# A planned attention and mixture kernel: the order of issue read from a table, and other engines for the last evictions

## The chip, the cores and the metric

The kernel runs on one core of a Trainium2 chip. The metric is the device time of one execution in microseconds (us), taken as the median of several runs; lower is better.

## The reference

Two parts follow each other. The first is attention over B = 8 batches, 8 heads, 576 positions and 64 elements a head. It is the sum of a full attention over queries, keys and values averaged over groups of four positions (144 of them, each result repeated four times), and a banded attention in which a position sees only those less than four away:

```
out_d    = softmax(scale * q_d @ k_d^T) @ v_d        # q_d, k_d, v_d: means over 4 positions
out_up   = repeat(out_d, 4)
scores   = where(|i - j| < 4, scale * q @ k^T, -1e9)
x        = (out_up + softmax(scores) @ v)  as (4608, 512)
```

The second part takes x (4608 tokens of 512) through four matrices:

```
out = ((x @ w1) * (x @ w2)) @ w3 @ w_out     # w1, w2: 512x1024, w3: 1024x1024, w_out: 1024x512
```

The four weight matrices arrive as 64-bit floating-point words.

## The kernel before

**The weights.** A weight block is loaded as raw 64-bit words (`raw`, 512 KB a load) and turned into 32-bit numbers on chip: ScalarE writes the high part (L355) and mostly also prepares the low one (L363; in a part of the blocks VectorE does it, L367), VectorE joins them (L370). w3 and w_out are multiplied once at the start: `product(m, j)` (into `accw`, L408) builds the folded matrix `wphl`, kept as a high and a low part (L429, L430). In the listings, `wo` is w_out, and `w_163`, `w_174`, `w_229` and so on are blocks of w3. `gate_block` converts w1 and w2 in the same way and splits them (L466, L468).

**The matmuls of the second part.** A product of numbers split in high and low is made with three matmuls (`three`, L323 to L325). `moe(c)` handles a chunk of 384 tokens, twelve chunks in all. For each of eight f blocks, four tasks of six matmuls give the two gates in `pab`; ScalarE copies the first (`a`, L1010), VectorE multiplies it with the second (L1012), ScalarE and VectorE split the result (`gh` L1017, `gl` L1019), and three tasks of three matmuls (`down`) add it to three accumulators `acc`. At the chunk's end ScalarE evicts the accumulators into `o_sb` (L1029), and SyncE's queue stores them (L1044 or L1046). In the last chunk ScalarE evicts the first half of each accumulator's columns, VectorE the second half (L1031), and the middle store is issued from ScalarE's queue.

**The attention.** The tokens come in 24 units of 192. For batches 0 and 1 (`group_unit`, `group_scores`, `group_values`) TensorE computes the banded scores. For the others `unit(n)` works on VectorE and ScalarE: loads of q, k and v (`q_t`, `kv`), seven shifted products (`pr`, L863) and their sums (`s_t`, L876 on VectorE, L873 on ScalarE), a softmax, seven weighted values (`pv`), added up in `xl` by VectorE (L940) or by an accumulating DMA from GpSimd's queue (L938). The pooled attention is `pooled_sums` or `pooled` (which loads averages with further accumulating DMAs from GpSimd, L505), then `quad`: scores on TensorE (`s_ps`, L566), softmax (`pexp`, L581 to L600), a turn on TensorE (`t_ps`, `pt`, L609 to L618) and the values (`o_ps`, L527). The unit's result is split into `xh` and `xl` for the gates.

**What sets the order.** Every step is recorded as a task by `Plan.add`, with its engine, an assumed cost, its dependencies and the buffers (rings) that it takes and uses. `Plan.order` then simulates the engines with these costs, forwards and backwards, many times, keeps the best sequence, shifts the priorities of some groups by a list of numbers (`SHIFTS`), and returns one global order. The program is emitted in it, and each engine executes its own tasks strictly in that order. The three DMA queues used are those of SyncE, GpSimd and, once at the end, ScalarE. A load on SyncE's queue waits, by the semaphores it is given in turn, for the one issued eight loads before it. The first four weight loads are put ahead of all other loads by `AHEAD`.

Of the kernel before, what the change touches and what calls it, by code (L numbers as in the profile page):

```python
# [20 lines left out]
DM, DF = 512, 1024  # L21
# [21 lines left out]
NC = NU // 2  # L43
# [16 lines left out]
DEPTH = dict(PE=0.0)  # L60
SLACKS = (0.0, 0.1, 0.3, 0.6)
SLOW = [(slow, spare) for spare in (0.22, 0.5) for slow in (1.0, 1.1, 1.2)]
VARY = 0.03
RARE = 0.003
SEEDS = 4
ROUNDS = 8
AHEAD = 4

SHIFTS = [
    "gates.8.2:2 gates.9.5:-15.5",  # L70
    "down.0.1:-10 down.0.4:21.5 down.0.5:47.5 down.0.7:-65 down.1.1:-12 down.1.5:2 down.11.2:-4.5 down.2.0:-1"
    " down.2.2:-2 down.2.3:-11.5 down.2.4:-7.5 down.2.5:-46.5 down.3.2:-14.5 down.3.3:8.5 down.3.6:-11"
    " down.3.7:-29.5 down.4.4:-7 down.4.6:-10 down.5.4:14 down.6.4:-36 down.6.5:5 down.6.6:2.5 down.6.7:-52"
    " down.7.4:-19 down.7.7:1.5 down.8.4:3.5 down.8.5:74 down.9.2:3 down.9.3:-24 gate_block.0.0.0:-5.5"
    " gate_block.0.1.0:-21 gate_block.0.1.1:-15.5 gate_block.1.0.2:-20.5 gate_block.1.1.0:-26.5"
    " gate_block.1.1.2:-6.5 gates.0.0:-14 gates.0.1:-4 gates.0.2:-3.5 gates.0.5:-6 gates.1.1:1 gates.1.3:2"
    " gates.1.6:-2.5 gates.2.0:4.5 gates.2.1:-11.5 gates.2.2:2.5 gates.2.3:-3 gates.2.4:-3 gates.2.5:0.5"
    " gates.3.1:-7 gates.3.2:-30 gates.3.5:-31 gates.3.7:-16.5 gates.4.0:-20.5 gates.4.1:-29 gates.4.2:-14"
    " gates.4.4:1.5 gates.5.2:3.5 gates.5.3:0.5 gates.5.6:-3 gates.5.7:-1.5 gates.6.0:2 gates.6.2:-19.5 gates.6.3:-2"
    " gates.6.6:-1 gates.7.1:1.5 gates.7.6:-0.5 gates.8.3:2.5 gates.8.7:3 gates.9.6:-31.5 group_scores.0.2.0:4"  # L80
    " group_scores.0.2.1:3.5 group_scores.1.0.1:4.5 group_scores.1.1.0:-3 group_values.1:-14 group_values.2:3"
    " out_weight.3:-1 out_weight.4:3 out_weight.6:14 part.6.1:10.5 pooled.0:2.5 pooled.1:4.5 pooled.3:5.5"
    " pooled.4:3.5 pooled.6:11 pooled_sums.1:2.5 product.4.5:-6 product.7.0:7 product.7.1:4 quad.1.0:10.5"
    " quad.2.0:-6 quad.2.1:1 quad.3.0:-4.5 quad.3.1:-1 quad.4.0:1.5 quad.4.1:1 quad.6.0:0.5 quad.7.0:-7.5 rest.0:-1"
    " rest.1:-21.5 unit.11:-1 unit.13:1 unit.14:1 unit.16:1 unit.17:-4.5 unit.20:0.5 unit.21:2 unit.22:-0.5"
    " unit.23:7 unit.6:-1 unit.7:-0.5",
]
# [24 lines left out]
class Plan:  # L112
# [28 lines left out]
    def link(self):  # L141
        at = {t: i for i, t in enumerate(self.tasks)}
        self.pre, self.suc, self.then = [], [[] for _ in self.tasks], [[] for _ in self.tasks]
        for i, t in enumerate(self.tasks):
            l = sorted({at[d] for d in t.deps} | {at[d] for r in t.rings for d in r} - {i})
            self.pre.append(l)
            for d in l:
                self.suc[d].append(i)
            for d in t.after:
                self.then[at[d]].append(i)  # L150

    def run(self, prio, slack, back=False, slow=1.0, spare=0.22):


        tasks = self.tasks
        pre, suc = (self.suc, self.pre) if back else (self.pre, self.suc)
        n = len(tasks)
        left, can = [len(l) for l in pre], [0.0] * n
        if not back:
            left = [a + len(t.after) for a, t in zip(left, tasks)]  # L160
        start, end, order = [0.0] * n, [0.0] * n, []
# [1019 lines left out]
```

## Time and profile before

| | us |
|---|---|
| median of three runs | 768.3 |
| the runs | 767.92, 768.3, 769.8 |
| profiled execution, span | 769.4 |
| TensorE busy (PE) | 741.0 |
| VectorE busy (DVE) | 618.4 |
| ScalarE busy (ACT) | 524.4 |
| GpSimd busy (POOL) | 153.2 |

For the profiled execution the page gives its span alone, from the first to the last instruction; no other time of it is recorded. Busy times are sums over an engine's instructions; weight loads of TensorE (PEld) run beside its matmuls. Times in the rows of the profile are counted from the start of the span. In a row of instructions, the brackets at the end give the idle time of the engine in front of it, and what ended it. SPq, ACTq and POOLq are the DMA issues of SyncE, ScalarE and GpSimd. The profiled execution is 1.1 us longer than the median.

### The profile page before, as it was taken

To read this page: it belongs to the slowest core of one execution; us is meant where nothing else is said; L and a number is where in the kernel's file an instruction comes from. 1 tells how busy PE (TensorE), PEld (TensorE's weight loads), DVE (VectorE), ACT (ScalarE), POOL (GpSimd) and SP (SyncE) were. 2 spreads that over 40 slices of the span, in tenths; PEclk is the share of its full clock that TensorE was granted. 3 is DMA by queue.
4 is the path that set the end of the run, shared out by engine and by line. 5 is a ranking of instruction groups with operands and counts; after the bars stand their busy time and mean duration, and the time that the engine had idled before them with its cause. 6 is when DMAs were issued, how large, how long until landed. Compare 5 with 4: busy or idle time off the path is not lost.

```text
span 769.4 us, 14989 instructions
## 1 busy us (share of the span) xinstructions
PE 741.0 (96%) x5248; PEld 639.5 (83%) x5248; DVE 618.4 (80%) x1079; ACT 524.4 (68%) x2074; POOL 153.2 (20%) x187
## 2 busy tenths in 40 slices
PE   4989999999999999999999899999999999999996
PEld 1435578889988999899998798999997998999995
DVE  5567887658999999999996999999989999973111
ACT  4579689557877877877787687776786886842211
POOL 1120031301012412141030422420223320100000
PEclk9999999999999999999999999999999999999998
DMA  8896768515249757876469568764469544331101
GB/s 305 286 273 203 231 143 212 111 36 195 52 125 237 147 126 200 156 155 179 88 153 208 91 169 216 131 177 118 100 167 223 118 115 124 66 78 21 42 1 41
DMA packets 46051, 111.91 MB, mean 145 GB/s; under 512 B 6280, under 2 KB 12424, under 8 KB 45976
## 3 DMA queue, kind: packets, MB, share of 16 engines
q0 software_dynamic: 15360, 38.94, 29.6%
q1 hardware_dynamic: 30480, 71.75, 28.6%
q8 instruction: 41, 0.67, 0.4%
q14 instruction: 34, 0.28, 0.1%
q10 hardware_dynamic: 136, 0.26, 0.1%
HBM read 80.26 MB, written 9.44 MB: 117 GB/s over the span
## 4 chain that ended last, share of the span: by engine, by line
PE 79%; DMA 8%; DVE 6%; ACT 4%; issue 2%; POOL 0%; ACTq 0%; SPq 0%; DVEq 0%; POOLq 0%
PE pab L323 15%; PE pab L325 15%; PE pab L324 15%; PE acc L323 8%; PE acc L324 7%; PE acc L325 7%; DMA raw<-in_w_dram 4%; PE accw L408 4%; DMA kv<-in_kw_dram 2%; PE o_ps L527 1%; DVE pr L863 1%; PE s_ps L566 1%; PE t_ps L609 1%; ACT junk L873 1%; DMA xl<-pv 1%
## 5 line engine op out<-in xcount | busy, mean ns | idle before, releaser
L873 ACT ACTIVATE junk<-pr 128x64 f32<-128x64 f32 x432 | 111.1, 257 | 23.1 <-DVE pr L863 12.1
L863 DVE TENSOR_TENSOR pr<-q_t,kv 128x768 f32<-128x768 f32 x126 | 119.6, 967 | 4.1 <-DMA kv<-in_kw_dram 3.7
L922 ACT ACTIVATE pv<-kv,s_t 128x64 f32<-128x64 f32 x432 | 110.9, 338 | 11.5 <-DVE s_t L899 5.9
L323 PE MATMUL acc<-wphl,gh 128*128 128x512 f32 x288 | 114.4, 397 | 0.0
L325 PE MATMUL acc<-wphl,gl 128*128 128x512 f32 x288 | 113.2, 393 | 1.2 <-DVE gl L1019 1.2
L324 PE MATMUL acc<-wphl,gh 128*128 128x512 f32 x288 | 112.7, 391 | 0.0
L938 POOL DMA_DIRECT2D xl<-pv x54 | 48.3, 895 | 298.5 <-DVE xl L940 211.2
L1010 ACT COPY a<-pab 128x384 f32<-128x384 f32 x96 | 45.8, 477 | 71.6 <-PE pab L325 56.2
L1012 DVE TENSOR_TENSOR a<-pab,a 128x384 f32<-128x384 f32 x96 | 53.1, 553 | 48.2 <-PE pab L325 46.4
L876 DVE TENSOR_REDUCE s_t<-pr 128x12 f32<-128x768 f32 x90 | 84.1, 946 | 0.4
L1017 ACT CAST gh<-a 128x384 fp32r<-128x384 f32 x96 | 48.9, 510 | 47.3 <-PE acc L324 41.2
L873 ACT ACTIVATION_READ_ACCUMULATOR junk<-pr 128x1 f32 x432 | 81.1, 188 | 0.0
L408 PE MATMUL accw<-wo,w 128*128 128x512 f32 x128 | 64.5, 642 | 13.4 <-DVE w L370 12.8
L1019 DVE TENSOR_TENSOR gl<-a,gh 128x384 fp32r<-128x384 f32 x96 | 54.2, 566 | 27.6 <-ACT gh L1017 25.9
L930 DVE TENSOR_TENSOR pv<-kv,s_t 128x768 f32<-128x768 f32 x72 | 69.5, 969 | 0.1
L323 PE MATMUL pab<-xh,w1a 128*128 128x384 f32 x192 | 66.1, 344 | 2.2 <-ACT a L1010 1.9
L323 PE MATMUL pab<-xh,wb 128*128 128x384 f32 x192 | 65.4, 341 | 2.3 <-ACT a L1010 2.2
L323 PE MATMUL pab<-xh,wo 128*128 128x384 f32 x192 | 65.9, 343 | 0.0
L323 PE MATMUL pab<-xh,w2a 128*128 128x384 f32 x192 | 65.3, 340 | 0.3 <-DVE a L1012 0.3
L325 PEld LDWEIGHTS acc<-wphl,gl 128*128 128x128 f32 x288 | 54.0, 188 | 13.5 <-DVE gl L1019 1.6
L324 PE MATMUL pab<-xl,w1a 128*128 128x384 f32 x192 | 64.9, 338 | 0.2 <-DVE xl L810 0.2
L325 PE MATMUL pab<-xh,wo 128*128 128x384 f32 x192 | 64.8, 337 | 0.0
(118 smaller groups left out, 1726.8 us busy)
## 6 DMA issues: line engine op xcount, KB each, us to landing
xl<-pv POOLq DMA_DIRECT2D x54, 384.0 KB, 4.3
raw<-in_w_dram SPq DMA_DIRECT2D x32, 512.0 KB
qks<-in_qk_dram POOLq DMA_DIRECT2D x18, 576.0 KB, 7.6
kv<-in_kw_dram SPq DMA_DIRECT2D x18, 576.0 KB
kv<-in_vw_dram SPq DMA_DIRECT2D x18, 576.0 KB
out_dram<-o_sb SPq DMA_DIRECT2D x29, 256.0 KB
q_t<-in_q_dram SPq DMA_DIRECT2D x18, 384.0 KB
raw<-in_wout_dram SPq DMA_DIRECT2D x8, 512.0 KB
```

The costliest lines, as they stand in the source:

```text
L323: nc.tensor.matmul(out_ps, lhsT=lh, rhs=rh, start=first, stop=False)
L324: nc.tensor.matmul(out_ps, lhsT=lh, rhs=rl, start=False, stop=False)
L325: nc.tensor.matmul(out_ps, lhsT=ll, rhs=rh, start=False, stop=last)
L408: nc.tensor.matmul(accs[m], lhsT=T["x"][:, j % 4 * 128:j % 4 * 128 + 128], rhs=wo[0][:, j], start=j == 0, stop=j == NF - 1)
L863: (nc.gpsimd if o in share["qk_pool"] else nc.vector).tensor_tensor(out=T[o], in0=T["q"], in1=T["k"][:, o * D:o * D + nq].rearrange("p (t ...
L873: nc.scalar.activation(out=junk, in_=T[o][:, t], func=AF.Copy, accum_out=T["s"][:, t, o:o + 1])
L876: reds.append(add("DVE", dve_us(nq), lambda o=o: nc.vector.tensor_reduce(out=T["s"][:, :, o], in_=T[o], op=ALU.add, axis=AX.X), [tp], uses ...
L922: nc.scalar.mul(out=T["pv", o][:, tt], in_=T["v"][:, (tt + o) * D:(tt + o + 1) * D], mul=T["s"][:, tt, o:o + 1])
L930: nc.vector.tensor_tensor(out=T["pv", o], in0=T["v"][:, o * D:o * D + nq].rearrange("p (t d) -> p t d", d=D), in1=T["s"][:, :, o].unsqueez ...
L1012: tg = add("DVE", dve_us(CT), lambda f=f: nc.vector.tensor_tensor(out=T["a", f], in0=T["p", 1, f], in1=T["a", f], op=ALU.mult), [ta, ends[ ...
L1017: nc.scalar.copy(out=T["gh", f], in_=T["a", f])
L1019: tl = add("DVE", dve_us(CT), lambda f=f: nc.vector.tensor_tensor(out=T["gl", f], in0=T["a", f], in1=T["gh", f].bitcast(F32), op=ALU.subtr ...
```

## The change

The search is gone. A table, `ORDER`, holds for each engine the sequence in which it takes its tasks, as numbers into the list of tasks that the plan recorded for that engine; `order` merely merges the five sequences. `AHEAD` is gone too, but the table keeps the first four weight loads in front. In `moe`, the eviction of an accumulator depends on the last matmul into that accumulator (`ended[i]`), where it was the last into the third for all; the three evictions are recorded ahead of the three stores. In the last chunk the first and third accumulators are evicted whole by ScalarE, the second whole by VectorE, and the middle store, still on ScalarE's queue, also waits for the third eviction, and so is issued behind it.

```diff
-AHEAD = 4
-SHIFTS = [
-    "gates.8.2:2 gates.9.5:-15.5",
...
+ORDER = dict(
+    ACT=(
+        "76 75 78 77 79 81 80 82-83 0 2-3 84 1 86 6 85 5 87-88 7 4 8-9 89 91 90 93 92 10 13 12 14-15 11 94 18 16-17 21 20 19 96 95 97-98 "
...
     def order(self):
+
+        self.link()
+        mine, left, free, end, dma, order = {}, {}, {}, {}, 0.0, []
...
+        while any(left.values()):
+            can = []
+            for e in sorted(left):
+                if left[e] and all(j in end for j in self.pre[left[e][-1]] + self.begun[left[e][-1]]):
+                    can.append((max([free[e]] + [end[j] + (0.22 if self.tasks[j].eng == "PE" else LATENCY) for j in self.pre[left[e][-1]] if self.tasks[j].eng != e]), e))
+            s, e = min(can)
+            i = left[e].pop()
...
             if t.late:
+                dma = max(dma, free[e] + 1.3) + t.late
+                end[i] = dma + 0.8
+            order.append(t)
+        return order
...
+                ended[i] = lastd
...
+        last = c == NC - 1
+        kept = []
         for i in range(3):
-            def store_h(i=i):
+            def keep(i=i):
                 T["o", i] = pools["mp"].tile([128, DM], F32, name="o_sb", bufs=BUFS["o"] + 1)
-                own = DM // 2 if c == NC - 1 else DM
-                nc.scalar.copy(out=T["o", i][:, :own], in_=T["acc"][i][:, :own])
-                if own < DM:
-                    nc.vector.tensor_copy(out=T["o", i][:, own:], in_=T["acc"][i][:, own:])
-            t, ho = add("ACT", act_us(DM, psum=True), store_h, [lastd] + (late if c == 0 else []), take=[R["o"]], uses=[hacc])
-
+                if last and i == 1:
+                    nc.vector.tensor_copy(out=T["o", i], in_=T["acc"][i])
+                else:
+                    nc.scalar.copy(out=T["o", i], in_=T["acc"][i])
+            en, cost = ("DVE", dve_us(DM)) if last and i == 1 else ("ACT", act_us(DM, psum=True))
+            kept.append(add(en, cost, keep, [ended[i]] + (late if c == 0 else []), take=[R["o"]], uses=[hacc]))
+        for i, (t, ho) in enumerate(kept):
             def store(i=i):
                 lo = i * 128
-                queue = nc.scalar if c == NC - 1 and i == 1 else nc.sync
+                queue = nc.scalar if last and i == 1 else nc.sync
...
-            add("SP", 0.5, store, [t], uses=[ho], late=dma_us(128 * 2048))
+            add("SP", 0.5, store, [t] + [k for k, _ in kept[2:] if last and i == 1], uses=[ho], late=dma_us(128 * 2048))
...
-    first = [t for t in plan.tasks if t.eng == "SP" and t in weight_loads][:AHEAD]
```

The order changes in many places of every engine. Three are shown; lines of the kernel after the change have lower numbers, since the search is gone from the file.

SyncE's queue at the start, before the change: `raw` are weight loads, q and k those of the pooled sums, `v_w` pieces of v for the banded attention of batches 0 and 1.

```order
L348 DMA raw<-in_w_dram 128x1024 x2
L348 DMA raw<-in_wout_dram 128x1024
L644 DMA q_145<-in_qk_dram 128x4x144
L673 DMA k_147<-in_qk_dram 128x288 x4
L644 DMA q_154<-in_qk_dram 128x4x144
L673 DMA k_156<-in_qk_dram 128x288 x4
L348 DMA raw<-in_w_dram 128x1024
L702 DMA v_w<-in_v_dram 18x512 x4
L348 DMA raw<-in_wout_dram 128x1024
L348 DMA raw<-in_w_dram 128x1024
L702 DMA v_w<-in_v_dram 18x512 x4
L644 DMA q_201<-in_qk_dram 128x4x144
```

The same place after the change:

```order
L324 DMA raw<-in_w_dram 128x1024 x2
L324 DMA raw<-in_wout_dram 128x1024
L620 DMA q_145<-in_qk_dram 128x4x144
L620 DMA q_147<-in_qk_dram 128x4x144
L649 DMA k_149<-in_qk_dram 128x288 x4
L649 DMA k_157<-in_qk_dram 128x288 x4
L678 DMA v_w<-in_v_dram 18x512 x12
L620 DMA q_203<-in_qk_dram 128x4x144
L678 DMA v_w<-in_v_dram 18x512 x4
L620 DMA q_217<-in_qk_dram 128x4x144
L324 DMA raw<-in_w_dram 128x1024
L324 DMA raw<-in_wout_dram 128x1024
```

The fifth weight load, the third block of w3, stood behind ten loads of q and k and now stands behind 28 loads of q, k and v; the sixth follows it at once.

TensorE at the start, before the change (a row of L408 is one product, which the trace shows as two matmuls; `x2` are two products):

```order
L408 MATMUL accw_177<-wo,w_163 128x512
L408 MATMUL accw_178<-wo,w_174 128x512
L408 MATMUL accw_177<-wo,w_163 128x512
L408 MATMUL accw_178<-wo,w_174 128x512
L408 MATMUL accw_179<-wo,w_229 128x512 x2
```

And after it:

```order
L384 MATMUL accw_175<-wo,w_164 128x512
L384 MATMUL accw_176<-wo,w_172 128x512 x2
L384 MATMUL accw_175<-wo,w_164 128x512
L542 MATMUL s_ps<-qks 64x144 x8
L384 MATMUL accw_177<-wo,w_259 128x512 x2
```

The scores of the first quad now stand between the four products with the first two blocks of w3 and those with the third.

SyncE's queue in the middle of the program, around the loads of unit 15, before the change (`qks` is a load of pooled inputs, `out_dram` are stores of a finished chunk):

```order
L850 DMA kv<-in_vw_dram 128x1152
L486 DMA qks<-in_qk_dram 128x1152
L1046 DMA out_dram<-o_sb 8x16x512
L1046 DMA out_dram<-o_sb 4x16x512 x2
L1046 DMA out_dram<-o_sb 8x16x512
L842 DMA q_t<-in_q_dram 128x768
L846 DMA kv<-in_kw_dram 128x1152
L850 DMA kv<-in_vw_dram 128x1152
```

After the change:

```order
L826 DMA kv<-in_vw_dram 128x1152
L1027 DMA out_dram<-o_sb 8x16x512
L1027 DMA out_dram<-o_sb 4x16x512 x2
L462 DMA qks<-in_qk_dram 128x1152
L1027 DMA out_dram<-o_sb 8x16x512
L822 DMA kv<-in_kw_dram 128x1152
L818 DMA q_t<-in_q_dram 128x768
L826 DMA kv<-in_vw_dram 128x1152
```

The load of pooled inputs has moved behind three of the four stores, and the unit's k (L846, now L822) stands ahead of its q.

More of the change, by code (lines that the diff above doesn't have):

```diff
@@ L1 @@
-import random
 from contextlib import ExitStack
@@ L59 @@
 LATENCY = 0.09
[L60 to L66, printed above, removed]
-AHEAD = 4
-SHIFTS = [
-    "gates.8.2:2 gates.9.5:-15.5",
[L71 to L87, printed above, removed]
+ORDER = dict(
+    ACT=(
[29 rows of a table added]
+    ),
+    DVE=(
[30 rows of a table added]
+    ),
+    PE=(
[17 rows of a table added]
+    ),
+    Pool=(
[5 rows of a table added]
+    ),
+    SP=(
[4 rows of a table added]
+    ),
+)
 LOWS = dict(early=('ACT', 'ACT', 'DVE'), late=('ACT', 'DVE'))
@@ L212, in replay @@
-    def replay(self, order, seed):
-        rng, tasks = random.Random(seed), self.tasks
-        end, free, dma = [0.0] * len(tasks), {}, 0.0
-        for i in order:
-            t = tasks[i]
-            x = free.get(t.eng, 0.0)
-            for j in self.pre[i]:
-                f = tasks[j].eng
-                x = max(x, end[j] + (DEPTH.get(f, 0.04) if f == t.eng else 0.22 if f == "PE" else LATENCY))
-            x += t.cost if t.eng in ("PE", "SP") else t.cost * (1 + abs(rng.gauss(0, VARY))) + (rng.random() < RARE)
-            free[t.eng] = x
-            if t.late:
-                dma = max(dma, x + 1.3) + t.late * (1.05 + abs(rng.gauss(0, 2 * VARY)))
-                x = dma + 0.8 + rng.random()
-            end[i] = x
-        return max(end)
@@ L230, in again @@
[L230 to L233 removed]
+        self.pre = [sorted({at[d] for d in t.deps} | {at[d] for r in t.rings for d in r} - {i}) for i, t in enumerate(self.tasks)]
+        self.begun = [[at[d] for d in t.after] for t in self.tasks]
     def order(self):
         self.link()
[L239 to L263 removed]
@@ new lines, in order @@
+        mine, left, free, end, dma, order = {}, {}, {}, {}, 0.0, []
+        for i, t in enumerate(self.tasks):
+            mine.setdefault(t.eng, []).append(i)
+        for e, l in mine.items():
+            left[e] = [l[k] for w in ORDER[e].split() for a, _, b in [w.partition("-")] for k in range(int(a), int(b or a) + 1)][::-1]
+            free[e] = 0.0
+            assert sorted(left[e]) == l
+        while any(left.values()):
[5 more added lines that the diff above has]
+            i = left[e].pop()
+            t = self.tasks[i]
+            free[e] = end[i] = s + t.cost
+            if t.late:
+                dma = max(dma, free[e] + 1.3) + t.late
+                end[i] = dma + 0.8
+            order.append(t)
@@ L970, in moe @@
         lastd = None
+        ended = {}
         lag = []
@@ L1072, in tile_attention_moe @@
             moe(n // 2)
-    first = [t for t in plan.tasks if t.eng == "SP" and t in weight_loads][:AHEAD]
-    for t in plan.tasks:
-        if t.eng == "SP" and t not in weight_loads:
-            t.after.extend(first[-1:])
     order = plan.order()
```

92 lines of the change are left out of this document (removed), and 84 rows, old and new, of tables (ACT, DVE, PE, Pool).

## The prediction

> **What bounds the kernel now.** I read the page's busy line first, then a table of stretches, then the waits of TensorE, and last the instructions around each wait. From the page, the span and the busy time by engine:
>
> ```profile
> span 769.4 us, 14989 instructions
> PE 741.0 (96%) x5248; PEld 639.5 (83%) x5248; DVE 618.4 (80%) x1079; ACT 524.4 (68%) x2074; POOL 153.2 (20%) x187
> ```
>
> TensorE is the bound: 741.0 of 769.4, and the change takes no matmul away. So all that can be won is among the 28.4 us in which TensorE is not busy. The table of stretches says where they lie (columns: stretch, then busy us of PE, its weight loads, DVE, ACT, POOL, the granted clock, DMA share, GB/s):
>
> ```profile
> 0.00:20.00 20.00, 8.75 (x11) 3.23 (x12) 11.16 (x32) 7.76 (x12) 3.67 (x19) 0.94 0.89 302
> 20.00:40.00 20.00, 18.66 (x88) 7.95 (x87) 11.37 (x31) 11.32 (x29) 2.67 (x3) 0.97 0.89 286
> 40.00:60.00 20.00, 17.91 (x97) 8.27 (x101) 11.27 (x22) 15.55 (x38) 4.90 (x6) 1.00 0.96 272
> 80.00:100.00 20.00, 18.68 (x171) 11.03 (x169) 17.11 (x41) 12.96 (x27) 0.00 (x0) 1.00 0.74 226
> 100.00:120.00 20.00, 18.98 (x130) 16.77 (x131) 16.06 (x37) 17.91 (x66) 8.35 (x10) 1.00 0.79 208
> 420.00:440.00 20.00, 17.98 (x105) 15.90 (x104) 17.05 (x22) 12.87 (x61) 8.94 (x11) 1.00 0.51 96
> 176.00:652.00 476.00, 472.18 (x3046) 431.21 (x3045) 448.04 (x704) 361.40 (x1563) 119.23 (x132) 1.00 0.64 150
> 760.00:769.40 9.40, 1.81 (x8) 1.16 (x7) 1.27 (x3) 1.12 (x3) 0.00 (x0) 0.78 0.27 84
> ```
>
> The losses are 14.7 in 0 to 60 (11.25 + 1.34 + 2.09), 2.3 in 80 to 120 (1.32 + 1.02), 3.8 in 176 to 652, 2.02 of it in 420 to 440, and 7.6 behind 760. VectorE is busy for 448 of the 476 us of the middle, 94%: whatever it waits for there is soon felt. TensorE's own waits name the releasers:
>
> ```profile
> PE accw L408 <- DVE w L370: 12.8, 4, 8.2
> PE pab L323 <- ACT a L1010: 4.1, 5, 2.0
> ```
>
> 8.2 of the 12.8 is the wait for the first weight block, which the change leaves in its place (the first four weight loads stay in front). The runs' median, 768.3, lies 1.1 below this execution's span; sums are made against the span, and 1.1 is taken off at the end.
>
> **Head, up to 107 us.** The first products of TensorE, what ended ScalarE's wait for the third block of w3, and SyncE's queue:
>
> ```profile
> 8.23 3.78 PE L408 MATMUL accw<-wo,w 128*128 128x512 f32 x4 [8.23 <-DVE w L370]
> 12.48 2.86 PE L408 MATMUL accw<-wo,w 128*128 128x512 f32 x4 [0.47 <-DVE wo L370]
> 17.89 8.29 PE L408 MATMUL accw<-wo,w 128*128 128x512 f32 x15 [2.54 <-DVE w L370]
> 15.90 0.67 ACT L355 ACTIVATE w<-raw 128x512 f32<-128x512 f32 x1 [5.74 <-DMA raw<-in_w_dram]
> 14.27 2.63 SPq L702 DMA_DIRECT2D v_w<-in_v_dram x4
> ```
>
> The new order puts 18 more loads on SyncE's queue ahead of that block: 16 pieces of v (36 KB) and two of q (288 KB), 1.18 MB. By bytes, at the 302 GB/s of the first stretch, the block lands 3.9 later; by issues, at 0.66 for a load (2.63 over 4), some 12 later. So its landing at 15.9 becomes 19.8 to 28. Followed load by load (in the program each waits for the eighth ahead of it) I come to 22, near the end by bytes, because the DMA engines are already 89% busy and the pieces mostly wait for the landings of larger loads. TensorE took 2.0 from landing to product (15.90 to 17.89), so the fifth product starts at about 24.0: 6.1 late. What is behind it on TensorE, all products with that block, is late with it; the four products ahead of it wait for nothing new.
>
> Three things give that back. One quad's scores stand in the gap now (16 matmuls, about 0.6 by the row of 36.37 below, 30 in 1.12). And the waits at 35 to 46 were these:
>
> ```profile
> 36.37 1.12 PE L566 MATMUL s_ps<-qks 64*64 64x144 f32 x30 [0.65 <-ACT pt L616]
> 40.65 1.98 PE L408 MATMUL accw<-wo,w 128*128 128x512 f32 x4 [1.25 <-DVE w L370]
> 43.60 1.09 PE L609 MATMUL t_ps<-ident,pexp 128*128 128x128 f32 x8 [0.57 <-ACT pexp L595]
> 45.49 0.70 PE L408 MATMUL accw<-wo,w 128*128 128x512 f32 x1 [0.80 <-DVE w L370]
> ```
>
> They sum to 3.27, and an engine that is behind, with the quads' pieces earlier in its order, meets inputs that are there. 6.1 - 0.6 - 3.3 leaves 2.2 behind at 45.5; followed instruction by instruction, the same work (24 products, four pieces of quads) ends at 46.3, 0.8 behind, since q and v no longer stand between the weights from 24 us on. The third thing lies at 93 to 107, where gate weights set the end:
>
> ```profile
> 100.14 0.45 PE L323 MATMUL pab<-xh,w1a 128*128 128x384 f32 x1 [1.00 <-ACT a L1010]
> 98.48 0.67 ACT L363 ACTIVATE raw<-raw 128x512 int32<-128x512 uint16 x1 [1.22 <-DMA raw<-in_w_dram]
> ```
>
> ScalarE sits in front of a conversion whose raw words have not landed (98.48), and the copy of the gate's result, queued behind it, comes late. These are ends in absolute time: a TensorE that arrives up to 2.3 later (1.32 + 1.02) loses nothing more. One product more (two matmuls) stands ahead of the first gates, too. So the head is 0.8 - 2.3 = -1.5 by the one count and 2.2 - 2.3 = -0.1 by the other; I take -0.8, with ends at -3 (0.8 + 2.2 better than taken: the waits of 35 to 46 go and nothing is late at 45) and +2.1 (the lag of 2.2 stays and the gate weights come later with it).
>
> The clock at this place:
>
> ```profile
> 17.69:21.10 3.41, 3.21 (x4) 1.51 (x5) 1.23 (x3) 1.72 (x3) 0.00 (x0) 0.50 0.66 177
> ```
>
> After the wait of 2.54 TensorE had half its clock for 3.4 us, 1.6 us lost. The new order has that spell once as well, behind its longer wait, and the sum has it on both sides. [...]
>
> **Middle.** At 425 TensorE loses 2.02. The rows, from SyncE's queue to it:
>
> ```profile
> 405.83 3.64 SPq L842 DMA_DIRECT2D q_t<-in_q_dram x1
> 409.53 0.83 SPq L846 DMA_DIRECT2D kv<-in_kw_dram x1
> 422.91 0.96 DVE L863 TENSOR_TENSOR pr<-q_t,kv 128x768 f32<-128x768 f32 x1 [3.67 <-DMA kv<-in_kw_dram]
> 426.96 0.48 ACT L1010 COPY a<-pab 128x384 f32<-128x384 f32 x1 [3.34 <-DVE gl L1019]
> 427.49 0.44 PE L323 MATMUL pab<-xh,wb 128*128 128x384 f32 x1 [2.02 <-ACT a L1010]
> ```
>
> Unit 15's k is held behind its q, whose issue took 3.64, and lands when VectorE has waited 3.67 for it; gl, the gate's copy and TensorE follow. The new order issues k ahead of q, behind one load of pooled inputs (576 KB) that stood before the stores and is now among them. 3.64 of issue is just the size of VectorE's wait, so I take 2.0 as gained; the moved pooled load, 2.8 us at 211 GB/s in other words, bounds it at 0. The other loss, at 578:
>
> ```profile
> 570.33 0.86 POOL L938 DMA_DIRECT2D xl<-pv x1 [4.61 <-DVE xl L940]
> 578.38 0.96 DVE L940 TENSOR_TENSOR xl<-xl,pv 128x768 f32<-128x768 f32 x1 [2.89 <-DMA xl<-pv]
> 579.86 0.50 PE L325 MATMUL acc<-wphl,gl 128*128 128x512 f32 x1 [1.20 <-DVE gl L1019]
> xl<-pv POOLq DMA_DIRECT2D x54, 384.0 KB, 4.3
> ```
>
> An add by DMA, 4.3 in the median, took 8.0 here, and VectorE had run out of other work. This place may go or stay: half of 1.2, so -0.6. But the new order also leaves less VectorE work between such an add and its need (23 instead of 17 of the 54 with under 6.5 us, counting the instructions of the two orders with the durations of these rows). On GpSimd's queue the accumulating loads of pooled inputs and these adds change places by one or two, which delays an add by at most an issue each (0.86). I put one such wait more, +1.2. The middle is -2.0 - 0.6 + 1.2 = -1.4, with ends at -3.8 (all of its loss) and +5 (four such waits of 1.2 beside a stall at 425 that is only moved).
>
> **Tail.** ScalarE evicts a half of each tile, VectorE the other half behind it; the second row is the last matmul:
>
> ```profile
> 760.49 0.37 ACT L1029 COPY o_sb<-acc 128x256 f32<-128x256 f32 x1 [2.17 <-PE acc L325]
> 761.42 0.39 PE L325 MATMUL acc<-wphl,gl 128*128 128x512 f32 x1
> 762.03 1.22 ACTq L1046 DMA_DIRECT2D out_dram<-o_sb x1
> 763.35 0.37 ACT L1029 COPY o_sb<-acc 128x256 f32<-128x256 f32 x1 [1.81 <-issue]
> 763.75 0.42 DVE L1031 COPY o_sb<-acc 128x256 f32<-128x256 f32 x1 [1.75 <-ACT o_sb L1029]
> GB/s 0 0 0 0 0 0 0 0 0 0 0 0 0 0 0 0 0 0 0 0 0 97 34 28 119 193 205 199 182 210 193 171 148 193 188 23 0 0 0 0
> L1029 ACT COPY o_sb<-acc 128x512 f32<-128x512 f32 x33 | 18.8, 581 | 0.5 <-PE acc L325 0.4
> ```
>
> The third half at 763.35 was free at about 761.8 and stood behind ScalarE's own issue of 1.22. Now ScalarE takes a whole tile (0.58 by the last row), VectorE the second at the same time (0.42 for a half, at most 0.84), ScalarE the third at about 761.83 to 762.41. So the last store is issued at 762.45 instead of 764.2: 1.75 earlier. But the GB/s row (40 slices of 0.36 from 755) shows the 0.79 MB going out at some 190 from 764 on without a hole: two stores that are issued together at 762.45 still have 0.52 MB to move, 2.8 us at that rate. If they can't overlap the first one, only its 0.2 earlier issue counts (0.58 for 0.37 + 0.42). -0.9, between -0.2 and -1.75. VectorE and ScalarE have nothing else left, so the added wait of the middle store for the third eviction delays only that store (762.03 to 762.45), and it is no longer the last. That the evictions of the other chunks wait for their own accumulator's last matmul instead of the third's costs and brings nothing: ScalarE waited 0.4 for TensorE ahead of all 33.
>
> **Sum.** -0.8 - 1.4 - 0.9 = -3.1: 766.3 against the span, 765.2 against the median, 0.4% faster.
>
> **Rivals.** First, more gain: head and middle at their good ends and the stores overlapping. -3 - 3.8 - 1.75 = -8.6, 759.7. For it: every wait named has a cause that the order touches. Against it: it needs no new wait in 3,300 rows of TensorE.
>
> Second, no difference: the weights come late, the clock is halved once more (+1.6), and the stores drain no earlier. +0.8 + 1.6 - 2.3 = +0.1 at 107, -1.4 in the middle, -0.2 at the end: 767.9 against the span, 766.8. For it: the row with 0.50 and the DMA share of 0.89. That the tail's change does nothing, its stores being bound by their rate, belongs here.
>
> Third, slower: VectorE's waits for the adds. At 578 a wait of 2.9 cost TensorE 1.2; with VectorE 94% busy, several in a row cost their full 2.9, since no slack is left to soak them up. From the forecast, it takes 5.4 more to be 0.3% slower (a measurement of this kernel tells about 0.3%, 2.3 us, from no change): two adds in full, or five at the price of 578. Two or three in full, 5.8 to 8.7, give 771 to 774. For it: less work behind 6 more of the adds. Against it: of 54 only one was felt before.
>
> **How the numbers follow.** My forecast 0.40 (its own range 762.5 to 767.5), more gain 0.14, no difference 0.24, slower 0.22. The forecast is faster by over 0.3% below 766.0, most of its range (0.32 of its 0.40); with 0.14 and 0.05 of the second rival that is 0.51. Slower: 0.22, less 0.02 that stay within 0.3%, with 0.02 of the second. Same: the rest, 0.27. The range leaves out the best half of the first rival's ground and the worst third of the last: 759.5 to 772.
>
> **What the profile after would show.** Right: the third block's conversion at about 22 instead of 15.9, the gap before TensorE's fifth product near 6 instead of 2.5, no waits of 0.5 or more at 35 to 46; no 2.0 at 425; last eviction ended by 762.5 minus what was gained before it, and the last stores issued together. Wrong: the fifth product later than 26, or a sum of VectorE's waits for xl<-pv over 6 between 176 and 652, which would make it slower; or the stretch 80 to 120 losing over 3.

## The result, and the profile after

The change makes the kernel slower: 774.81 us in the median of six runs (772.03 to 779.34), against 768.11 for the kernel before (767.06 to 770.39, six runs). The ratio is 1.0072, with a 95% interval of 1.0044 to 1.0101. Forecast were 765.2 and a range that ended at 772. The profiled execution took 776.16 us, 1.86 more than its span; by the same difference the profile of before shows an execution of about 771.2, some 3 us longer than its median, and not 1.1: a span is shorter than the time of its execution.

The busy line of the page of the kernel after:

```profile
span 774.3 us, 14935 instructions
PE 742.1 (96%) x5248; PEld 639.3 (83%) x5248; DVE 620.7 (80%) x1077; ACT 523.8 (68%) x2073; POOL 151.9 (20%) x187
```

The span is 4.9 longer: 1.1 of it is TensorE busy for longer with the same 5248 matmuls, 3.8 is TensorE idle. The table of stretches after, with the columns of the prediction:

```profile
0.00:20.00 20.00, 7.92 (x24) 2.75 (x24) 9.70 (x30) 5.87 (x9) 3.66 (x19) 0.91 0.75 239
20.00:40.00 20.00, 14.75 (x71) 6.80 (x64) 12.07 (x32) 11.59 (x30) 4.29 (x6) 0.83 0.97 310
40.00:60.00 20.00, 20.00 (x113) 9.33 (x111) 10.01 (x20) 15.14 (x39) 3.43 (x5) 1.00 0.92 282
80.00:100.00 20.00, 19.39 (x192) 11.27 (x192) 16.76 (x42) 13.05 (x30) 0.00 (x0) 1.00 0.72 224
100.00:120.00 20.00, 18.44 (x126) 16.37 (x126) 15.71 (x37) 16.66 (x60) 8.28 (x10) 1.00 0.67 161
120.00:176.00 56.00, 53.34 (x821) 45.32 (x820) 34.97 (x93) 39.06 (x136) 10.24 (x12) 1.00 0.53 120
300.00:400.00 100.00, 98.28 (x584) 89.18 (x587) 93.70 (x147) 73.28 (x312) 22.71 (x24) 1.00 0.60 141
420.00:440.00 20.00, 19.96 (x114) 17.56 (x114) 19.73 (x33) 14.81 (x59) 7.46 (x9) 1.00 0.77 161
176.00:652.00 476.00, 473.09 (x3059) 430.13 (x3058) 447.19 (x698) 357.79 (x1554) 116.88 (x132) 1.00 0.65 150
```

From 0 to 60 TensorE now loses 17.33 where it lost 14.68. From 120 to 176, where before it lost nothing, it loses 2.66; no term of the prediction stood there. The 2.02 at 425 are gone, but 1.72 are lost from 300 to 400 (0.07 before), so that the whole middle went only from 3.82 to 2.91. The waits of TensorE in the stretch 104 to 165 of the kernel after (line waited at, releaser, us in total, times, longest):

```profile
PE pab L299 <- ACT a L988: 2.1, 2, 1.3
PE se_ps L725 <- issue: 1.1, 1, 1.1
```

The first is 1.3 at 131 and 0.8 at 107: ScalarE's copy of a gate comes late. The second row is an odd one. "issue" means that TensorE waited for nothing that the profile shows, and the rows around it have it in the middle of a run of 24 short matmuls whose inputs were all there:

```profile
143.25 0.65 PE L725 MATMUL se_ps<-k,qn 64*64 64x72 f32 x22
144.96 0.35 PE L725 MATMUL se_ps<-k,qn 64*64 64x72 f32 x2 [1.06 <-issue]
```

In the profile of before the same 24 run through:

```profile
139.82 0.66 PE L749 MATMUL se_ps<-k,qn 64*64 64x72 f32 x24
```

The changed kernel was run a second time, beside the experiments below:

> The changed kernel unaltered, for a second profile and on the chip of the parts: 1.006 to 1.008. If the wait at 336 to 339 us (1.7 us of TensorE) belongs to the order, it is seen again; if it is a matter of one execution, as the wait at 425 us of the kernel before was (with the same sequences and the new tail the stretch 400 to 500 lost 0.58 instead of 2.36), it isn't.

It measured 1.0104 (1.0066 to 1.0143). Its profile (span 784.7) shows what 104 to 165 can cost in a long execution, and where. That execution, 786.51 us, was a slow one at a lower clock (0.984 in the mean, 0.986 to 0.998 in the others), the longest of seven (the others took 774.48 to 779.41) and not among those of the ratio, so its lengths are read as an extreme, beside those of after and of e9 below. The waits of TensorE there:

```profile
PE se_ps L725 <- issue: 3.7, 1, 3.7
PE t_ps L585 <- ACT pexp L571: 3.4, 1, 3.4
```

The place of the first, in TensorE's rows, and a stretch behind it in the columns of the table:

```profile
154.83 0.50 PE L725 MATMUL se_ps<-k,qn 64*64 64x72 f32 x2 [3.72 <-issue]
```

```profile
156.00:158.00 2.00, 2.00 (x8) 2.00 (x8) 0.72 (x2) 0.00 (x0) 0.46 (x1) 0.50 0.54 92
```

The wait stands ahead of the same two matmuls, 3.72 long, and half the clock (0.50) follows it. Two theories came of this. By the first, a copy of pooled inputs, `vl`, that VectorE takes too early holds it up (2.9 in the profile after, 7.5 here) and with it `pexp` and TensorE. By the second, the matter lies in TensorE's own stream of instructions, and in its clock.

### The profile page after: what moved, and what is told of

The parts are those of the page before. It is cut to its first block, busy times and chain, and to the rows that moved or that the text cites. A ratio compares the mean times of both kernels' runs of the same rounds, so it can differ in the third digit from the quotient of the medians.

```text
span 774.3 us, 14935 instructions
## 1 busy us (share of the span) xinstructions
PE 742.1 (96%) x5248; PEld 639.3 (83%) x5248; DVE 620.7 (80%) x1077; ACT 523.8 (68%) x2073; POOL 151.9 (20%) x187
## 4 chain that ended last, share of the span: by engine, by line
PE 67%; DMA 11%; issue 7%; DVE 7%; ACT 4%; SPq 2%; POOL 2%; POOLq 0%; DVEq 0%; ACTq 0%
PE pab L299 13%; PE pab L301 13%; PE pab L300 13%; PE acc L299 6%; PE acc L301 6%; PE acc L300 6%; DMA raw<-in_w_dram 5%; PE accw L384 5%; DMA vl<-in_v_dram 3%; DVE pr L839 2%; DMA qks<-in_qk_dram 1%; PE o_ps L503 1%; PE s_ps L542 1%; DVE s_t L852 1%; DMA vs<-in_v_dram 1%
## 5 line engine op out<-in xcount | busy, mean ns | idle before, releaser
L300 PE MATMUL pab<-xl,wo 128*128 128x384 f32 x192 | 64.7, 337 | 0.0
```

Of the source, the lines that this page charges most:

```text
L300: nc.tensor.matmul(out_ps, lhsT=lh, rhs=rl, start=False, stop=False)
```

## The experiments

All are the code of the kernel after with another table, or with a few matmuls more; "old" and "new" are the sequences of before and of after, "head" is what stands ahead of the first gates (to about 93 us). Ratios are to the kernel before, run on the same chip.

**Which part of the order.** In e1 all five engines have the old sequences, with the new tail; e2 adds the new head; e3 is old up to the second chunk's gates (about 174 us) and new behind them; e4 is old in the head and new behind it; e5 is new between the two gates alone; e6 is e2 with the old sequence on SyncE's queue.

```diff
-ORDER = dict(ACT=new, DVE=new, PE=new, Pool=new, SP=new)
+ORDER = dict(ACT=old, DVE=old, PE=old, Pool=old, SP=old)      # e1
+# e2: tasks ahead of "gates 0 0" as new, the rest as old
+# e3: tasks ahead of "gates 1 0" as old, the rest as new
+# e4: tasks ahead of "gates 0 0" as old, the rest as new
+# e5: ahead of "gates 0 0" old, up to "gates 1 0" new, the rest old
+# e6: e2 with SP=old
```

> Each engine's sequence is that of the kernel before, with the new code for the last three evictions and the middle store alone. The forecast's tail: 0.9 us less (0.2 to 1.75). The trace after, measured from the last matmul to the end of the span (7.53 for 7.98): 0.45 less, about 767.6. If the order of issue has no other effect than through its sequences, nothing else changes: no difference from the kernel before beyond this.

Measured 0.9998 (0.9981 to 1.0015): the tail by itself brings nothing that can be told.

> All tasks ahead of the first gates (to about 93 us) stand in the new order, the rest in the old, with the new tail. Theory A (the loss is made at the start, by the third block of w3 landing 7.5 late, and what is left of it at the first gates, 2.1, isn't given back): 2.1 - 0.45 = 1.7 slower than before, about 769.8. Theory B, the forecast's step (the waits for gate weights at 93 to 107 end at times of their own and absorb a lag of up to 2.3): 0.4 less than before, 767.7.

1.0044 (1.0021 to 1.0068): against e1 the new head costs some 3.5 us (0.0046 of 768). In the two profiles the first gate matmul starts 4.42 later in e2, the 48th 3.03 later: most of what the head loses stays.

> All tasks ahead of the second chunk's gates (to about 174 us) stand in the old order, the rest in the new, with the new tail. By the trace after, the middle loses 0.9 less than before and the tail 0.45: if all the loss lies ahead of 176, 1.3 faster than before, 766.8. Theory C (the new order's middle is what costs, through waits for adds by DMA such as that at 336): not faster, 2 or more slower, 770 or above.

1.0022 (1.0003 to 1.0040): what lies behind 174 us gains nothing, and the gain of the middle is not there. In its profile TensorE waits for "issue" ahead of the same two matmuls as in after, although all up to 174 us stands in the old order (TensorE's row of e3):

```profile
142.11 0.29 PE L635 MATMUL se_ps<-k,qn 64*64 64x72 f32 x2 [2.55 <-issue]
```

> All tasks ahead of the first gates stand in the old order, the rest in the new, with the new tail. If the 2.7 lost anew between 100 and 176 (waits at 125, 130 and 144) come from the order of that stretch itself, the time is 2.7 - 0.9 - 0.45 = 1.3 slower than before, 769.4. If they only follow from the late start, they vanish: 1.3 faster than before, 766.8, as the run with all tasks up to 174 in the old order.

1.0062 (1.0038 to 1.0085), in two groups of runs: 770.1 to 770.8 (three), and 773.3 and more (nine). The loss is not in the head alone, and what costs it behind the head happens in some executions only. The profiled one, 770.14, is of the low group, and its TensorE shows no wait of the kind "issue" from 104 to 165.

> Only the tasks between the first gates and the second chunk's gates (about 95 to 174 us) stand in the new order; head and rest in the old, new tail. The pair with the tasks up to 174 in the old order (1.0022) and only the head in it (1.0062) puts 0.004, 3 us, on this stretch. Theory A (the stretch's own order costs this, by its waits): 1.004, some 3 us slower than before. Theory B (it costs only together with the new order behind 174): within 0.15% of before. The first load of a unit's k or q on SyncE's queue, at 171.6 before and 178.6 after, should come at 174.5 by A.

1.0103 (1.0060 to 1.0146). This kernel has a seam of its own: TensorE waits 2.79 at 180 for ScalarE, which neither kernel does. It does not price the stretch.

> The kernel with the new head (1.0044), but SyncE's sequence is the old one, so that the third block of w3 stands behind ten loads instead of 28; TensorE, VectorE and ScalarE keep the new head. Theory A (the loads ahead of that block cost it): the fifth product at about 18 instead of 24.7, the first gates at about 92 to 93.5 instead of 96.2, and the time of the run with the new tail alone, 0.9998. Theory B (the head's cost lies in the order of VectorE and TensorE): 1.004 as with the whole new head.

1.0141 (1.0107 to 1.0175), the worst of all. The third block's conversion is back at 15.90, as before the change, yet the product that needs it is not (rows of e6: ScalarE, three of VectorE, TensorE):

```profile
15.90 0.67 ACT L241 ACTIVATE w<-raw 128x512 f32<-128x512 f32 x1 [5.76 <-DMA raw<-in_w_dram]
21.61 0.64 DVE L536 COPY qn<-q 128x576 f32<-128x576 f32 x1 [4.21 <-DMA q<-in_qk_dram]
25.22 0.31 DVE L547 TENSOR_TENSOR qks<-q 128x144 f32<-128x144 f32 x1 [2.07 <-DMA q<-in_qk_dram]
27.61 0.69 DVE L256 SCALAR_TENSOR_TENSOR w<-w,raw 128x512 int32<-128x512 int32 x1
28.36 2.08 PE L294 MATMUL accw<-wo,w 128*128 128x512 f32 x2 [7.32 <-DVE w L256]
```

VectorE's new order has the sums of q ahead of the join of that block; with q loaded as late as before it waits 4.21 and 2.07 for them while the weights lie ready. The order of a queue and that of the engine which it feeds belong together; with VectorE's new order, SyncE's new order is the better one.

**The first theory: vl.** In e9 VectorE takes the copy of `vl` ten tasks later.

```diff
-    DVE: "... 152 201 211-213 168 78-79 71 80 72-73 153 ..."
+    DVE: "... 152 211-213 168 78-79 71 80 72-73 201 153 ..."
```

> The changed kernel, with one task of VectorE moved: the copy of vl for the pooled values of batch 1 stands ten tasks later, behind the second quad's softmax and the masked scores, so that its wait for GpSimd's accumulating load (2.9 and 7.5 us in the two profiles of the changed kernel, 4.7 with the old head, none where the stretch is in the old order) holds up nothing of these. Theory A (that wait makes the stretch from 95 to 174 dear): 3 us or more less, 1.004 for 1.007 to 1.010. Theory B (the late start and the clock make the loss): unchanged.

1.0089 (1.0056 to 1.0123), no better. VectorE no longer waits for `vl`, and the "issue" wait is still there, ahead of the same two matmuls (e9, TensorE's rows), with a granted clock of 0.50 from 150 to 152 behind it:

```profile
142.53 0.65 PE L635 MATMUL se_ps<-k,qn 64*64 64x72 f32 x22
147.50 0.50 PE L635 MATMUL se_ps<-k,qn 64*64 64x72 f32 x2 [4.32 <-issue]
```

The loss is there without the wait for `vl`.

**The second theory: the clock.** In the head of after TensorE stops twice, and each time has half its clock behind it (TensorE's rows of after, then two stretches in the columns above):

```profile
15.86 3.65 PE L384 MATMUL accw<-wo,w 128*128 128x512 f32 x4 [3.31 <-DVE wo L346]
25.41 7.00 PE L384 MATMUL accw<-wo,w 128*128 128x512 f32 x11 [5.25 <-DVE w L346]
```

```profile
16.00:18.00 2.00, 2.00 (x3) 0.97 (x4) 1.09 (x3) 0.00 (x0) 0.00 (x0) 0.50 0.39 90
26.00:28.00 2.00, 2.00 (x3) 0.67 (x2) 1.14 (x4) 1.88 (x6) 0.00 (x0) 0.50 1.07 348
```

Each gap is followed by a clock of 0.50 in this execution. By the first theory filling them changes little; by the second it gives back the loss.

e7 (the sequences of e2) and e10 (those of after) fill the two gaps with ten long matmuls into an accumulator that is overwritten afterwards: the added work is thrown away. e11 is e9 and e10 together.

```diff
+                if (m, j) == (2, 0):
+                    for _ in range(7):
+                        nc.tensor.matmul(accs[2], lhsT=xs[1, 0][0]["x"][:, :128], rhs=wo[0][:, 0], start=True, stop=True)
                 nc.tensor.matmul(accs[m], lhsT=T["x"][:, j % 4 * 128:j % 4 * 128 + 128], rhs=wo[0][:, j], start=j == 0, stop=j == NF - 1)
+                if (m, j) == (1, 0):
+                    for _ in range(3):
+                        nc.tensor.matmul(accs[2], lhsT=xs[1, 0][0]["x"][:, :128], rhs=wo[0][:, 0], start=True, stop=True)
```

> The kernel with the new head (1.0044), with ten more matmuls on TensorE that are thrown away (into the accumulator that the third block of w3 starts afresh): three behind the first two products, seven ahead of the fifth. They fill the gaps of 3.3 and 5.3 us and do nothing else. If the clock is halved by such gaps, the fifth to eighth products take 0.43 a matmul instead of 0.85, and 1.5 of the lag goes: first gates at 94.5 to 95 instead of 96.2, ratio 1.0025. If the weights that follow set the pace anyway, the time stays at 1.0044; if dummies run over, the third product comes later than 15.5 and nothing is won.

0.9993 (0.9969 to 1.0016), from 1.0044 without them: clear of noise, but the ten matmuls also move all that follows, which is taken up below.

> The changed kernel with the ten thrown-away matmuls that took the new head on the old rest from 1.0044 to 0.9993. Theory B (the clock, halved for two windows at 16 to 29 us, 5.1 us in the first 30, and the lag that follows): 3 to 4 us less, 1.003 to 1.005. Theory A (the stretch from 95 on has an end of its own that a faster head doesn't move, as with the old head, 1.0062): less than 1.5 us.

1.0000 (0.9977 to 1.0023), from 1.0072 and 1.0104. Its stretches in the head:

```profile
0.00:20.00 20.00, 11.38 (x35) 4.75 (x36) 10.52 (x32) 5.87 (x9) 3.67 (x19) 1.00 0.77 249
20.00:40.00 20.00, 18.89 (x77) 8.14 (x76) 12.12 (x31) 12.24 (x33) 3.58 (x4) 1.00 0.97 306
```

The clock is 1.00 where it was 0.91 and 0.83. And VectorE waits for `vl`, in the row of its waits:

```profile
DVE vl L401 <- DMA vl<-in_v_dram: 4.4, 1, 4.4
```

That is more than the 2.9 in after, and the loss is gone all the same: with e9 this lets the first theory fall.

> Both of these edits. If the two causes add up: 6 to 7 us less than the changed kernel, 1.000. If they are one (the copy waits only because the head is late): no better than the better of the two.

0.9988 (0.9963 to 1.0014): with the clock kept, the moved copy brings nothing more.

**Clock or place in the stream.** Ten matmuls more do a second thing: all that follows stands 40 of TensorE's recorded instructions later (in the rows each counts as two matmuls, and each of these has a weight load). Counted in its stream, the wait at `se_ps` is at recorded instruction 2241 or 2242 in all six profiles that have it (after, e1, e2, e3, e8, e9); a small one at times at 1218, 1024 = 4 x 256 earlier; and in the six kernels with ten matmuls more there is none at 2242, but in five of them (all but e10) one at 961 or 962, which is 256 before 1218. So e13 puts ten short matmuls (32 x 8) in the same places, which move the stream alike but do not keep the clock up (6.8 us without clock in the mean of e13's runs, 2.1 in that of e10); e14, e15 and e16 do so to e5, e4 and e1 (three in e16), and e17 has e4's sequences with three long ones.

```diff
-                        nc.tensor.matmul(accs[2], lhsT=xs[1, 0][0]["x"][:, :128], rhs=wo[0][:, 0], start=True, stop=True)
+                        nc.tensor.matmul(accs[2][:32, :8], lhsT=xs[1, 0][0]["x"][:, :32], rhs=wo[0][:, 0, :8], start=True, stop=True)
```

> The changed kernel with ten thrown-away matmuls at the same places as in the run that took it to 1.000, but of 32 columns by 8, too short to keep the clock up. They move all later instructions of TensorE by as many places. Theory F (TensorE waits, at the same matmul of its stream, number 1097, for something that no semaphore shows: 1.1, 3.7 and 4.3 us in three profiles of the new order; the longer matmuls helped because they moved that place to another time): the time falls nearly as far, 1.000 to 1.003, while the clock is halved at 16 to 29 us as before. Theory B (the clock): 1.007 to 1.010.

1.0021 (0.9996 to 1.0046). Most of the loss of after is gone. In this profile the clock is still halved in the head (0.54 from 24 to 26, behind the gap of the second row), though for 3.4 us only where it was for 10.2 in that of after; over all runs the time without clock is the same as in after, 6.8 against 6.6 (table below), so the clock does not explain the gain. TensorE's rows of e13, the first one seven of the short matmuls, counted as 14:

```profile
20.21 0.82 PE L296 MATMUL accw<-wo,w 128*32 128x8 f32 x14
24.58 7.75 PE L297 MATMUL accw<-wo,w 128*128 128x512 f32 x14 [3.55 <-DVE w L256]
78.92 0.40 PE L641 MATMUL se_ps<-k,qn 64*64 64x72 f32 x2 [2.19 <-issue]
```

The wait has moved to 78.92. From 104 to 165 all that TensorE waits is one row:

```profile
PE o_ps L419 <- DMA vs<-in_v_dram: 0.8, 1, 0.8
```

The 1.06 of after and the 3.72 of e8 at 2242 are not there.

> The kernel with only the head in the old order (1.0062; its twelve runs stand in two groups, three near 770.5 and eight near 775), with the same ten short matmuls. Theory F: the upper group goes, 1.001 to 1.002. Theory A: unchanged.

0.9989 (0.9965 to 1.0012), from 1.0062, and the upper group of runs is gone (768.75 to 772.18). In e4's profile, of the lower group, the clock is 1.00 from 0 to 60 already, so in the head there was little for it to win. Over all runs both parts fall: the time without clock from 4.9 to 3.1, the rest from 769.3 to 767.2. The place in the stream is the likely cause, less cleanly than in e13.

> The kernel with only the stretch from 95 to 174 us in the new order (1.0103), with the same ten short matmuls. Theory F: 1.003 or below. Theory A (the stretch's waits themselves): unchanged, 1.008 or more.

1.0063 (1.0033 to 1.0092), from 1.0103 (1.0060 to 1.0146): perhaps part goes, but the two intervals overlap too far to tell, and the seam at 180, again 2.79, stays.

> The old sequences with the new tail and three short matmuls in the place of the three long ones that gave 0.9966. Theory F: 0.9966 to 0.998, since moving the place is what gains. Theory B: 0.9998, as without them.

0.9984 (0.9957 to 1.0012), against 0.9998 of e1: no difference that can be told, and none against the 0.9966 with three long ones (e12 below) either.

> The old head and the new order behind it, with the new tail and three long thrown-away matmuls ahead of the fifth product. With ten short ones the same order gave 0.9989, 5.6 us less than without. If moving the place of the wait is what counts, three (6 matmuls, 12 of TensorE's instructions) should do as well as ten when no boundary falls behind a run of short matmuls; the clock adds up to 1.6: 0.997 to 0.999. If three don't move it far enough: 1.006 as without.

1.0002 (0.9973 to 1.0031), in two groups again, 767.5 to 769.8 (seven) and 772.6 to 774.4 (five); with three matmuls more the stream stands elsewhere than in e4 and e15. What sets its upper group was not profiled.

**A better version.** e12 and e18 are the same kernel, run on two chips: old sequences, new tail, and three long matmuls in the one gap of the old head.

```diff
+                if (m, j) == (2, 0):
+                    for _ in range(3):
+                        nc.tensor.matmul(accs[2], lhsT=xs[1, 0][0]["x"][:, :128], rhs=wo[0][:, 0], start=True, stop=True)
```

> The old sequences with the new tail, and three thrown-away matmuls in the gap of 2.5 ahead of the fifth product, which keep the clock up: 1.6 of half clock at 17.7 to 21.1 goes, the waits at 36 to 46 for weights take back up to 3.3. Taken as half of it: 0.8 less than before and the tail's 0.1 to 0.4: 0.9985. If all is taken back, 0.9998, as with the tail alone.

> The old order with the new tail and the same three long matmuls again (0.9966 in its first run), on the same chip as the run beside it: 0.996 to 0.9985. If the first was chance, 0.9998.

0.9966 (0.9944 to 0.9989) and 0.9968 (0.9942 to 0.9994): faster than the kernel before by about 2.6 us. The gap is full (e12, the first row has the three thrown-away matmuls), and 0 to 40 has the clock at 1.00:

```profile
15.24 2.74 PE L296 MATMUL accw<-wo,w 128*128 128x512 f32 x6
17.99 6.28 PE L297 MATMUL accw<-wo,w 128*128 128x512 f32 x14
```

Whether the clock or the place in the stream makes the gain is not separated: e16, with three short matmuls, has as little time without clock over its runs (2.6 against 2.7) and lies between e1 and e12.

**What the clocks of all runs say.** Each run lists its span and its mean granted clock; (1 - clock) x span, averaged over a kernel's runs, is the time that it ran without clock, the rest is all else:

| kernel | runs | without clock, us | rest, us |
|---|---|---|---|
| before, on the experiments' chips | 137 | 3.8 | 766.6 |
| after, both times (without the 786.51) | 12 | 6.6 | 769.2 |
| e13: after + 10 short | 12 | 6.8 | 765.5 |
| e10: after + 10 long | 12 | 2.1 | 768.7 |
| e1: old, new tail | 12 | 4.2 | 766.3 |
| e12, e18: old, new tail, 3 long | 24 | 2.7 | 765.8 |

(Standard errors of the rest are 0.2 for before, 0.4 to 0.8 for the others; the first row's chips differ by up to 1.1.) Against before, after has 2.8 more without clock and 2.6 more elsewhere. Moving the stream (e13) takes the second away and leaves the first. Keeping the clock as well (e10 against e13) wins 4.7 of clock, yet only 0.21% of time, 1.6 us, and the two intervals overlap. The rest of e10 is 3.2 above that of e13 although its stream is moved alike, so the columns are not two costs that add up: a likely reason, not tried, is that a product at half speed ahead of a block that is not there yet costs little, and what the clock wins there comes back as waiting.

## Why the prediction was wrong, step by step

**Signs that came true.** The third block's conversion was put at about 22 and the fifth product at 24.0, with a gap near 6:

```profile
23.43 0.67 ACT L331 ACTIVATE w<-raw 128x512 f32<-128x512 f32 x1 [12.83 <-DMA raw<-in_w_dram]
24.67 0.69 DVE L346 SCALAR_TENSOR_TENSOR w<-w,raw 128x512 int32<-128x512 int32 x1
```

It was 23.43, and the product started at 25.41 behind a gap of 5.25. From 40 to 60 TensorE had no wait at all, the stall at 425 went, 80 to 120 lost 2.17. Every sign listed for being right was met, none of those for being wrong, and the kernel was slower: none of them stood where the time went.

**Head, -0.8.** This term failed, in two ways. Of its two counts the one by waits (2.2 behind at 45) was right in this profile and the one followed instruction by instruction (0.8) was not: the product that started at 45.49 before starts at 47.71, and the first gate matmul 2.11 later than before. The step "a TensorE that arrives up to 2.3 later loses nothing more" failed. Over eleven profiles with the old head and eight with the new (e6 left out), the first gate matmul starts at 92.6 and 96.5 in the mean, the 48th at 102.6 and 105.9: the lag is 3.9, beyond either count, and only 0.6 of it is given back. The profile of before, 104.52 at the 48th, happened to be late there, which made its 2.3 look like a reserve. The clock was the other way: "the new order has that spell once as well" was wrong, it has it twice, since the gap ahead of the third product grew from 0.47 to 3.31. In after the clock was 0.50 from 15.84 to 19.26, behind that gap, and from 22.67 to 29.50, which begins within the gap of 5.25: 5.1 us without clock in the head, where before had 1.7 (0.50 from 17.69 to 21.10). The second rival had the sign of this, with 1.6 for one more spell of the size of that in before; these two profiles have 3.4 there, and the means over whole executions in the table above 2.8. The length of a gap alone does not tell it: behind the 2.54 of before the clock was 0.50, behind 2.88 ahead of the third product in e13 it was 1.00 (16 to 18). The end at +2.1 and the rival's +1.6 together, 3.7, come near e2's cost of about 3.5; the term taken was 4.3 below that cost. How much of it is the clock is not separated.

**Nothing for 107 to 176.** This is the step that was missing: a loss where the profile of before shows TensorE without a gap, and so no row to price it by. The "issue" wait was 1.06 in the profiled execution (beside 1.30 for ScalarE's copy), 3.72 and 4.32 with half the clock behind it in those of e8 and e9, and moving the stream won 0.5% to 0.8% of the whole (after to e13, e4 to e15). The third rival had the sign right with another mechanism, the adds by DMA, and it does not carry the loss: VectorE's waits for them were 5.2 in all, below the 6 at which the prediction would have had them decide. One was felt, 0.89 and 0.55 at TensorE at 338 and 339 (VectorE's row):

```profile
336.13 0.96 DVE L916 TENSOR_TENSOR xl<-xl,pv 128x768 f32<-128x768 f32 x1 [2.71 <-DMA xl<-pv]
```

That is one add of 54, as in before, and it is the wait that the middle's +1.2 was put in for.

**Middle, -1.4.** Each of its three parts happened, but the first was mis-sized and other waits came that had no term. Ten profiles have the old sequences behind 192 us (before, e1, e2, e5, e6, e7, e12, e14, e16, e18) and ten the new. In the means of what TensorE idles, the stall near 425 goes from 0.6 to 0 (415 to 436; VectorE waits for that k in eight of the ten old profiles, but the 2.02 of before was the largest loss), the one near 578 from 1.2 to 0.2 (560 to 592). In return, 300 to 400 goes from 0.07 to 1.13: VectorE waits 1.7 to 2.8 for the add near 336 in all ten new profiles. From 464 to 490 it goes from 0.2 to 0.65 and from 490 to 560 from 0.1 to 0.4, which nothing in the prediction had. Over 192 to 652 TensorE idles 2.5 in the mean with the old sequences and 2.9 with the new: -1.4 was +0.4.

**Tail, -0.9.** The mechanism was right and the size was not. The three evictions (ScalarE, VectorE, ScalarE) and the stores after:

```profile
765.84 0.59 ACT L1011 COPY o_sb<-acc 128x512 f32<-128x512 f32 x1 [2.40 <-PE acc L301]
766.52 0.69 DVE L1009 COPY o_sb<-acc 128x512 f32<-128x512 f32 x1 [2.50 <-PE acc L301]
767.20 0.58 ACT L1011 COPY o_sb<-acc 128x512 f32<-128x512 f32 x1 [0.77 <-PE acc L301]
767.24 1.22 ACTq L1027 DMA_DIRECT2D out_dram<-o_sb  x1
```

What the stores moved, in 40 slices of 0.36 us from 759.9:

```profile
GB/s 0 0 0 0 0 0 0 0 0 0 0 0 0 0 0 0 0 0 0 0 0 57 46 34 51 165 199 193 188 171 193 205 199 210 188 74 11 0 0 0
```

From the start of the last matmul to the end of the span it took 7.96 before and 7.57 after, and 7.84 to 7.89 in e1, e2, e12 and e16: 0.07 to 0.39 won, at the end of the range at which the stores are bound by their rate. The GB/s row has them at about 190 without a hole from 768.9 on. ScalarE's store is issued at 767.24, beside its third eviction and not behind it, since what it waits for by data is VectorE's tile.

**What is shown and what is not.** The runs show that the new head costs 3.5 us with the old order behind it (e2 against e1), and that the loss of after falls to 0.2% or to nothing when 40 instructions are put ahead on TensorE's stream, whether these keep the clock up (e10) or not (e13). The two costs do not simply add up: e13 still has the new head, and measures 1.0021 (0.9996 to 1.0046). What the clock of the head costs by itself is not shown: e10 against e13, 0.2%, and e7 against e12, which would leave 2.1 us for the head with the clock kept, both lie within the noise.

What the wait is for is estimated here from the traces. The page of after lists this queue (packets, MB, share of the DMA engines):

```profile
q8 instruction: 41, 0.67, 0.3%
```

In each of the twenty profiles it moves 41 packets of 16 KB, and the 10,496 recorded matmuls and weight loads of TensorE in before are 41 times 256 (with its 99 recorded semaphore and drain instructions, which the numbers of the stream count too, 41.4 times); so by the author's estimate it brings TensorE its instructions, 256 a packet. Count marks 256 apart in TensorE's stream, so that 962, 1218 and 2242 are among them. A packet begins from 43 instructions ahead of a mark to 256 behind it, and of some 800 times TensorE never passed the next mark sooner than 1.2 us behind that packet's end. All fifteen "issue" waits of 0.4 to 4.3 us in the traces stand at such a mark and end 1.2 to 1.6 us behind the end of a packet that began late. In after TensorE passed the mark ahead of 2242 at 139.75; the packet ran from 142.66 to 143.61, and the wait ended at 144.96. In e8 and e9 it began 5.4 and 6.0 behind that mark, in before 1.1 ahead of it, and there TensorE did not wait. The traffic by queue in e8 from 152.0 to 152.5, in its wait, has that packet beside GpSimd's loads:

```profile
q0 software_dynamic: 35, 0.05, 56.3%
q1 hardware_dynamic: 23, 0.04, 20.9%
q8 instruction: 1, 0.02, 13.1%
q14 instruction: 1, 0.01, 3.9%
```

Why a packet begins late in one execution and not in another is open, and so is why the new order suffers more. Its profiles do not show it more often: among those whose stream is not moved, the wait at 2242 stands in three of five with the old order there (1.93 in e1, 1.75 in e2, 2.55 in e3, none in before and e6) and in three of five with the new (after, e8 and e9, not e4 and e5), where it is longer at worst. That TensorE runs through the 256 instructions ahead of it in some 4 us while GpSimd's loads (queue q0) take most of the DMA engines' time is so in both orders: 3.84 us and 95.0% in before, 3.92 us and 66.5% in after. Why the wait at 78.92 costs e13 little was not tried. And e17's upper group of runs was not explained.

## What to carry to other kernels

A new order of issue is priced by more than the waits of one profile: each gap that it opens on TensorE is to be asked whether it halves the clock behind it (here the clock was 0.50 behind gaps of 2.54, 3.31 and 5.25, and 1.00 behind one of 2.88), and the size of a stall is to be taken from several executions before it is counted as a gain. Where TensorE waits for "issue" inside a run of short matmuls, count its instructions and look when the packets of its instruction queue come: a few matmuls more ahead of it moved the place here, with ten short ones from 2242 to 962 in e13. A few thrown away in the gap ahead of a late weight kept the clock at 1.00 here (e12, 0 to 40), and the tuned kernel with them was 0.34% and 0.32% faster in two runs.

## What was not expected of the hardware

A wait that the view of waits puts down to "issue" alone, at recorded instructions 962, 1218 and 2242 of TensorE's stream, which differ by multiples of 256: 0.4 to 4.3 us, different from execution to execution, ending each time 1.2 to 1.6 us behind the end of a late packet of the queue that the page calls "instruction". And with it the spread: the same kernel before took 766.2 to 777.6 over 28 runs on one chip, of which 4.3 in the mean were time without clock.
